# Block products for chunks 8 to 15 of the first MoE layer, and down-sampled attention in three groups of rows

## The chip, the cores and the metric

The kernel runs on one core of a Trainium2 chip. The metric is the device time of one execution, in microseconds (us), from the first to the last instruction of the program and what little lies around them. TensorE (PE) multiplies, ScalarE (ACT) and VectorE (DVE) do the element work, GpSimd (POOL) a few sums, SyncE (SP) issues every DMA.

## What is computed

```python
# q, k, v: [2 batches, 8 heads, 576 positions, 64]
q_d, k_d, v_d = means over 4 neighbouring positions          # 144 rows a head
out_d     = softmax(q_d @ k_d.T / 8) @ v_d                    # down-sampled attention
out_local = softmax(q @ k.T / 8 where |i - j| < 4) @ v        # window attention
x = (repeat(out_d, 4) + out_local) as [1152 tokens, 512]
h = x @ w_in                       # 512 -> 2048     first MoE layer
x = (h * tanh(softplus(h))) @ w_out                  # 2048 -> 512
g, val = x @ w_gate, x @ w_val     # 512 -> 1536     second MoE layer
out = (g * sigmoid(g) * val) @ w_out2                # 1536 -> 512
```

The weights come as 64-bit floats, the rest as 32-bit floats.

## The kernel before

All operations are first recorded in a `Plan`, each with its engines, its costs in us, its dependencies and a due time (`want`); `Plan.run` then lists them in time order by these costs, and that list is the order of the instructions on every engine. The table `STEER` shifts the due times of single operations. Nothing is reordered on the chip: each engine goes through its list and waits where an operand is not ready. Where PE has nothing ready in the plan before 95 us, `run` puts a filler matmul there (`warm`, 256 columns of a constant, its result unused).

**Attention.** Heads go in pairs: `p` 0 to 3 in batch `b`. `prep` loads `qk` (queries and keys), `vq` (values for the down-sampled part) and once a batch `qr` (the last 64 positions), transposes on PE and sums four neighbours. `down` is the down-sampled attention of a pair: `score` (PE), `mx`, `neg` (DVE), `exps` (ACT), `norm`, `weigh`, `turn` (PE transposes of the probabilities), `ev`, `values`, `keep`. The 144 rows of each of the two heads stood as two halves of 72 rows, so four groups on 72 partitions. `duo` is the window attention of two units of 192 tokens; there are twelve, its last PE step is `o_local`, and it needs the windows `vw` (`load_windows`, four loads of a set). `dma` allows six loads in flight (`DEPTH`): each waits for the sixth before it.

**Matrix products.** Every factor is split into a high and a low part, and each product is three matmuls (`mm3`: high by high, high by low, low by high). Tokens go in three pieces of 384 (`PIECES`). The 2048 columns of the first layer are 16 chunks of 128; `l1(f, i)` is chunk `f` on piece `i`: 4 x 3 matmuls of 384 columns. `convert` loads a weight chunk (`raw`) and turns 64-bit floats into the two parts in `wt` (8 buffers): `fold`, `field` on ACT, `join` on DVE, `hi` on either, `lo` on DVE. `mish` works on two or four chunks `H` at once and leaves `G`. `l2` multiplies four chunks by `w_out`, twelve groups a block, and sums into `yacc`. The order is chunks 0 to 7, `l2` of block 0, chunks 8 to 11, `l2` of block 1, chunks 12 to 15, and so on.

**Block products.** The second layer (`l3`) already takes its chunks in pairs, and pieces 0 and 1 by seven products of blocks instead of eight (`products`). For that `combine` makes two more weight tiles of a pair from sums of halves (`sw`), and `turn_tokens` makes four token tiles (`tok` and a part of `yb`) from differences of blocks. A product is 2 x 3 matmuls; `keep` and `add_` move and add its result. Piece 2 is done plainly.

Of the kernel before, what the change touches and what calls it, by code (L numbers as in the profile page):

```python
# [8 lines left out]
F32 = mybir.dt.float32  # L9
# [18 lines left out]
PC = 384  # L28
# [5 lines left out]
DEPTH = 6  # L34
FLIGHT = 5
STEER = {
# [62 lines left out]
class Op:  # L99
    def __init__(self, eng, fn, deps, want, new, use, table):  # L100
        self.eng, self.fn, self.want, self.new, self.use, self.table = eng, fn, want, new, use, table
        self.left, self.at, self.out, self.end = 0, 0.0, [], None
        self.rings = {id(x.ring): x.ring for x in self.new}.values()
        for d in deps:
            if d is not None:
                self.left += 1
                d.out.append(self)
        for x in self.use:
            x.left += 1


class Plan:
# [5 lines left out]
    REST, SHARE, REACH, LAND = 0.0, 1.3, 1.5, 0.5  # L118
# [11 lines left out]
    def run(self):  # L130
# [10 lines left out]
        while todo:  # L141
            later, ran = [], False
            for e in names:
# [33 lines left out]
                if e == "DVE" and free["POOL"] > now:  # L177
                    d *= self.SHARE
# [37 lines left out]
def attention_moe_kernel(  # L216
# [259 lines left out]
    def prep(b, p, w):  # L476
# [39 lines left out]
        l_v = [plan.add({E_SP: us_dma(288, 1024, 12)}, ld_v, [], w - 5, [vq])]  # L516
# [72 lines left out]
    def down(b, p, qkd, vd, o_d, o_v, w):  # L589
# [4 lines left out]
        ed = buf(wk, [72, 2, 2, SD], F32, "ed", 2)  # L594
        md = buf(wk, [72, 2, 2, 2], F32, "md", 3)
        ptd = buf(wk, [72, 2, 2, SD], F32, "ptd", 1)
        old = ups.get("op")

        def score(e):
            for y in ba + [ed, md]:  # L600
                y.make()
            for c in range(2):
                for h in range(2):
                    hh = slice(64 * h, 64 * h + 64)
                    PE.matmul(out=ba[h].tile[0:72, SD * c:SD * c + SD], lhsT=qkd.tile[hh, 0, 72 * c:72 * c + 72],  # L605
# [714 lines left out]
```

## Time and profile before

| | |
|---|---|
| median of 3 runs | 492.81 us (492.2 to 496.83) |
| profiled execution | 495.21 us, of it 493.4 us span |
| PE busy | 483.1 us, 98% of the span |
| DVE busy | 327.3 us, 66% |
| ACT busy | 267.7 us, 54% |

The span is from the first to the last instruction of the profiled execution. Busy shares are over the whole span; the stages differ, and the rows further down are read by stage.

### The profile page before, as it was taken

The numbers are of one execution on the slowest core, as the hardware profiler recorded it, in microseconds if no ns is written. First come the engines' busy times: TensorE is split into PE (matmuls) and PEld (weight loads), VectorE is DVE, ScalarE is ACT, GpSimd is POOL, SyncE is SP. The second block draws the span as 40 slices with busy tenths as digits, with TensorE's granted clock in tenths as the row PEclk, the third lists the DMA queues.
The fourth block names the chain that finished last, engine by engine and source line by source line (L and its number), as shares of the span: only waits on it lengthen the run. The fifth ranks groups of instructions, "written<-read, shape, count | busy, mean of one in ns | idle before, by whom it ended". The sixth has DMA issues, their size and how long they took to land.

```text
span 493.4 us, 9431 instructions
## 1 busy us (share of the span) xinstructions
PE 483.1 (98%) x3857; PEld 454.2 (92%) x3857; DVE 327.3 (66%) x634; ACT 267.7 (54%) x523; POOL 21.5 (4%) x41
## 2 busy tenths in 40 slices
PE   9999799999999999999999999999999999999996
PEld 6777589999999999999999999999998899998885
DVE  4989869639504643865578989798892298872522
ACT  3677668669627733867252775666661485730000
POOL 2333210000000000000000000000000000000000
PEclk9999979999999999999999999999999999999999
DMA  8999996622300640153111051423351042400022
GB/s 169 171 178 187 190 159 181 207 86 86 128 1 0 182 161 1 43 177 123 43 31 55 2 166 48 128 63 111 97 182 62 0 115 101 126 4 0 0 108 85
DMA packets 59993, 48.79 MB, mean 99 GB/s; under 512 B 32430, under 2 KB 55214, under 8 KB 59950
## 3 DMA queue, kind: packets, MB, share of 16 engines
q1 hardware_dynamic: 59950, 48.19, 38.0%
q8 instruction: 30, 0.49, 0.4%
q14 instruction: 13, 0.11, 0.1%
HBM read 45.83 MB, written 2.36 MB: 98 GB/s over the span
## 4 chain that ended last, share of the span: by engine, by line
PE 94%; DMA 4%; issue 1%; DVE 0%; SPq 0%
PE b L850 23%; PE b L852 23%; PE b L851 23%; PE b L1145 5%; PE b L1144 5%; PE b L1146 5%; DMA vw<-in_v_dram 3%; PE warm L1283 2%; PE b L789 2%; DMA qr<-in_k_dram 1%; PE b L540 1%; PE b L746 1%; PE b L605 1%; PE b L656 1%; PE b L776 1%; PE b L644 1%
## 5 line engine op out<-in xcount | busy, mean ns | idle before, releaser
L850 PE MATMUL b<-xy,wt 128*128 128x384 f32 x384 | 129.7, 338 | 0.0
L852 PE MATMUL b<-xy,wt 128*128 128x384 f32 x384 | 128.7, 335 | 0.0
L851 PE MATMUL b<-xy,wt 128*128 128x384 f32 x384 | 128.7, 335 | 0.0
L850 PEld LDWEIGHTS b<-xy,wt 128*128 128x128 f32 x384 | 72.3, 188 | 0.7 <-ACT cw L351 0.4
L851 PEld LDWEIGHTS b<-xy,wt 128*128 128x128 f32 x384 | 72.4, 189 | 0.0
L852 PEld LDWEIGHTS b<-xy,wt 128*128 128x128 f32 x384 | 72.3, 188 | 0.0
L852 PE MATMUL b<-G,wt 128*128 128x384 f32 x192 | 64.7, 337 | 0.0
L850 PE MATMUL b<-G,wt 128*128 128x384 f32 x192 | 64.6, 336 | 0.0
L851 PE MATMUL b<-G,wt 128*128 128x384 f32 x192 | 64.3, 335 | 0.0
L272 ACT ACTIVATE H<-b 128x384 f32<-128x384 f32 x60 | 29.3, 488 | 59.0 <-PE b L852 58.8
L358 DVE SCALAR_TENSOR_TENSOR cw<-raw,cw 128x512 uint32<-128x512 uint32 x68 | 46.5, 685 | 13.2 <-ACT cw L355 12.7
L351 ACT ACTIVATE cw<-raw 128x512 f32<-128x512 int8 x68 | 45.3, 667 | 17.9 <-DVE wt L372 12.5
L372 DVE TENSOR_TENSOR wt<-cw,wt 128x512 fp32r<-128x512 f32 x68 | 46.2, 685 | 5.5 <-ACT wt L272 4.0
L274 DVE CAST wt<-cw 128x512 fp32r<-128x512 f32 x29 | 12.3, 423 | 51.4 <-PE b L851 31.9
L355 ACT ACTIVATE cw<-cw 128x512 int32<-128x512 f32 x68 | 42.7, 628 | 1.0
L1145 PE MATMUL b<-wt,G 128*128 128x512 f32 x108 | 42.3, 392 | 0.0
L1144 PE MATMUL b<-wt,G 128*128 128x512 f32 x108 | 42.2, 391 | 0.0
L1146 PE MATMUL b<-wt,G 128*128 128x512 f32 x108 | 42.1, 390 | 0.0
L851 PEld LDWEIGHTS b<-G,wt 128*128 128x128 f32 x192 | 36.0, 188 | 0.0
L850 PEld LDWEIGHTS b<-G,wt 128*128 128x128 f32 x192 | 36.0, 188 | 0.0
L852 PEld LDWEIGHTS b<-G,wt 128*128 128x128 f32 x192 | 36.0, 188 | 0.0
L965 DVE TENSOR_TENSOR acc<-b,acc 128x384 f32<-128x384 f32 x36 | 19.6, 553 | 23.7 <-PE b L852 23.7
(108 smaller groups left out, 743.0 us busy)
## 6 DMA issues: line engine op xcount, KB each, us to landing
raw<-in_moe_w_out_dram SPq DMA_DIRECT2D x28, 512.0 KB
raw<-in_moe_w_in_dram SPq DMA_DIRECT2D x16, 512.0 KB
raw<-in_moe_w_gate_dram SPq DMA_DIRECT2D x12, 512.0 KB
raw<-in_moe_w_val_dram SPq DMA_DIRECT2D x12, 512.0 KB
vw<-in_v_dram SPq DMA_DIRECT2D x14, 189.0 KB
vq<-in_v_dram SPq DMA_DIRECT2D x8, 288.0 KB
out_dram<-acc SPq DMA_DIRECT2D x9, 256.0 KB
qk<-in_q_dram SPq DMA_DIRECT2D x8, 256.0 KB
```

The source lines that it names most:

```text
L272: ACT.activation(out, in_, AF.Copy)
L351: ACT.activation(cw.make(), raw.tile[:, 8:4104].bitcast(I8).rearrange("p (n b) -> p n b", b=8)[:, :, 0], AF.Prelu, scale=-1.0, bias=-56.0, ...
L355: ACT.activation(cw.tile.bitcast(I32), cw.tile, AF.Prelu, scale=-2.0 ** 27 / SLOPE, bias=-112 * 2.0 ** 27, alpha=SLOPE)
L358: DVE.scalar_tensor_tensor(out=cw.tile.bitcast(U32), in0=raw.tile[:, 0:4096].bitcast(U32).rearrange("p (n b) -> p n b", b=2)[:, :, 1], sca ...
L372: DVE.tensor_tensor(out=wt.tile[:, 1], in0=cw.tile, in1=wt.tile[:, 0].bitcast(F32), op=ALU.subtract)
L850: PE.matmul(out=ps, lhsT=wt_hi, rhs=m_hi, start=first, stop=False, **more)
L851: PE.matmul(out=ps, lhsT=wt_hi, rhs=m_lo, start=False, stop=False, **more)
L852: PE.matmul(out=ps, lhsT=wt_lo, rhs=m_hi, start=False, stop=last, **more)
L965: DVE.tensor_tensor(out=ya, in0=ps.tile[:, 0:n], in1=ya, op=ALU.add)
L1144: PE.matmul(out=ps.tile, lhsT=g[:, 0, tok], rhs=wt[:, 0], start=(f == fs[0]), stop=False)
L1145: PE.matmul(out=ps.tile, lhsT=g[:, 0, tok], rhs=wt[:, 1], start=False, stop=False)
L1146: PE.matmul(out=ps.tile, lhsT=g[:, 1, tok], rhs=wt[:, 0], start=False, stop=(f == fs[-1]))
```

## The change

Chunks 8 to 15 of the first layer (`PAIRS = 8`) go in four pairs by seven products on pieces 0 and 1 (`l1_pair`), with the same `products` as the second layer, now told where its tokens are. `turn_x` makes the four token tiles: it adds the two parts of `x` back together (four DVE additions of 768 columns into the buffer `acc`), subtracts (four), and splits again (four `hi`, four `lo`); one of the four overwrites piece 1 of two rows of `x`, once chunks 0 to 7 have read it. Each pair of chunks has its `combine`. In `down`, the 288 rows of the two heads now stand in three groups of 128 partitions: 80 rows of the first head, then its other 64 beside 64 of the second head, then the second head's other 80. The first and the third group carry 48 rows that nothing reads. The load of `vq` is two transfers, of 64 and of 8 partitions. `STEER` and the plan's cost of sharing (`SHARE`, now on four kinds of DVE operations alone) are other numbers.

```diff
+PAIRS = 8
-    REST, SHARE, REACH, LAND = 0.0, 1.3, 1.5, 0.5
+    REST, SHARE, REACH, LAND = 0.0, 1.5, 1.5, 0.5
+    SHARED = ("norm_l", "x_lo", "lo", "join")
...
-            dma(out=vq.make().rearrange("p h c f -> p (h c) f"),
-                              in_=bass.AP(tensor=s_.tensor, offset=s_.offset, ap=[[4 * D, 72], [2 * SD * D, 4], [1, 4 * D]]))
+            vq.make()
+            for r, n in ((0, 64), (64, 8)):
+                dma(out=vq.tile.rearrange("p h c f -> p (h c) f")[r:r + n],
+                    in_=bass.AP(tensor=s_.tensor, offset=s_.offset + 4 * D * r, ap=[[4 * D, n], [2 * SD * D, 4], [1, 4 * D]]))
...
-            for h in range(2):
-                for c in range(2):
-                    ACT.activation(ed.tile[:, h, c], ba[h].tile[0:72, SD * c:SD * c + SD], AF.Exp, bias=md.tile[:, 0, h, c:c + 1],
-                                   scale=1.0 / 16.0, accum_out=md.tile[:, 1, h, c:c + 1])
+            for g in range(3):
+                ACT.activation(ed.tile[:, g], group(g), AF.Exp, bias=md.tile[:, 0, g:g + 1], scale=1.0 / 16.0, accum_out=md.tile[:, 1, g:g + 1])
...
-                for a in range(2):
-                    for c in range(2):
-                        PE.transpose(out=ba[h].tile[0:72, SD * a + 72 * c:SD * a + 72 * c + 72], in_=ed.tile[:, h, c, 72 * a:72 * a + 72],
-                                     identity=ident[:72, :72])
+                for g, (a, n) in enumerate(rows):
+                    PE.transpose(out=ba[h].tile[0:72, a:a + n], in_=ed.tile[0:n, g, 72 * h:72 * h + 72], identity=ident[:n, :n])
...
+    def turn_x(want):
...
+        for x, (r, c) in enumerate(((0, 0), (0, 1), (1, 1), (1, 0))):
+            def back(e, x=x, r=r, c=c):
+                if x == 0:
+                    xacc.make()
+                hi, lo = [xt[:, z, 2 * r:2 * r + 2, (p0, p1)[c]].bitcast(F32) for z in range(2)]
+                DVE.tensor_tensor(out=part(x), in0=hi, in1=lo, op=ALU.add)
...
+        for x, a, b in ((0, 1, 0), (1, 2, 1), (2, 2, 0), (3, 3, 2)):
+            def sub_(e, x=x, a=a, b=b):
+                DVE.tensor_tensor(out=part(x), in0=part(a), in1=part(b), op=ALU.subtract)
...
+            later = [] if t else reads
+            o = plan.add({"ACT": us_act(2 * PC), "DVE": us_ts(2 * PC)}, hi, [subs[k]] + later, want, [t] if t else [], [xacc] + ([] if t else [x_buf]))
+            xtok_ops.append(plan.add({"DVE": us_tt(2 * PC)}, lo, [o] + later, want, use=[xacc, t or x_buf]))
...
+    def l1_pair(f, want):
...
+        tokens = (x_buf, lambda: xt, raw, t, xtok_ops, [x_buf] + xtok)
+        pa, o4, c11, c12, c22 = products("1", f, want, hs, both, tokens)
+        tail = [cols_group("1", f + x, 2, lambda: xt, [o for p in range(NP) for o in x_ops[p, 2]], want + x, [x_buf]) for x in range(2)]
...
     def add_l1(fs):
+        if fs[0] >= PAIRS:
+            for f in fs[::2]:
+                groups.append(([("1", f, 2)], 5.82, lambda t, f=f: l1_pair(f, t)))
+            return
...
     add_l1((6, 7))
+    groups.append(((), 0, lambda t: turn_x(t - 12.0)))
```

**SP's list around the last loads of attention.** In the kernel before, from the last query load on (`qk` queries and keys, `vq` and `vw` values, `raw` weight chunks of the first layer):

```order
L279 DMA qk_143<-in_q_dram 128x8x64
L279 DMA vq_152<-in_v_dram 72x4x256
L279 DMA qk_143<-in_k_dram 128x8x64
L279 DMA vw_270<-in_v_dram 42x18x64 x4
L279 DMA vq_156<-in_v_dram 72x4x256
L279 DMA raw_1052<-in_moe_w_in_dram 128x4x1024
L279 DMA raw_1092<-in_moe_w_in_dram 128x4x1024
L279 DMA raw_479<-in_moe_w_in_dram 128x4x1024
L279 DMA vw_200<-in_v_dram 42x18x64 x3
```

The same place in the changed kernel:

```order
L281 DMA qk_143<-in_q_dram 128x8x64
L281 DMA qk_143<-in_k_dram 128x8x64
L281 DMA vw_578<-in_v_dram 42x18x64 x3
L281 DMA vw_316<-in_v_dram 42x18x64
L281 DMA vq_171<-in_v_dram 64x4x256
L281 DMA vq_171<-in_v_dram 8x4x256
...
L281 DMA raw_973<-in_moe_w_in_dram 128x4x1024
L281 DMA raw_1017<-in_moe_w_in_dram 128x4x1024
L281 DMA vw_316<-in_v_dram 42x18x64 x2
L281 DMA vw_316<-in_v_dram 42x17x64
...
L281 DMA vw_578<-in_v_dram 42x18x64 x4
```

Three windows `vw` and one `vq` that stood ahead of the last key load now stand behind it, and two weight chunks instead of three stand in front of the last windows (one more stands far ahead of this place in both).

**PE's list at the first matmuls of the first layer.** Before, behind the seventh of the twelve `o_local` (L789; L644 and L776 transposes, L605 scores of the down-sampled attention, `xy` the tokens):

```order
L789 MATMUL b_219<-pt_435,vw_270 64x32 x2
L776 MATMUL b_224<-ident,exs 128x128 x3
L605 MATMUL b_182<-qkd_234 72x144
L605 MATMUL b_193<-qkd_234 72x144
...
L850 MATMUL b_225<-xy_82,wt_734 128x384
L851 MATMUL b_225<-xy_82,wt_734 128x384
```

In the changed kernel, behind the sixth (L795; L742 and L752 scores of the windows):

```order
L795 MATMUL b_218<-pt_581,vw_578 64x32 x2
L742 LDWEIGHTS identb
L742 MATMUL b_181<-masks,identb 128x228
L752 MATMUL b_181<-qkT_211 32x38 x10
L752 MATMUL b_181<-qkT_211 32x35 x2
L856 MATMUL b_237<-xy_82,wt_688 128x384
L857 MATMUL b_237<-xy_82,wt_688 128x384
```

The first layer begins one window group earlier; up to the last `o_local` 120 of its matmuls stand instead of 72. In the whole list 84 fillers stand instead of 117, 48 transposes of `turn` instead of 64, and 1920 matmuls of 384 columns instead of 1944.

**DVE's list behind the last window group.** Before, from the last token split on (`xy<-xs`; L358 `join`, L372 `lo`):

```order
L813 TENSOR_TENSOR xy_82<-xs_696,xy_82 128x2x192
L358 SCALAR_TENSOR_TENSOR cw_1268<-raw_1052,cw_1268 128x512
L274 CAST wt_1532<-cw_1335 128x512
L372 TENSOR_TENSOR wt_1532<-cw_1335,wt_1532 128x512
L274 CAST wt_734<-cw_685 128x512
L372 TENSOR_TENSOR wt_734<-cw_685,wt_734 128x512
```

In the changed kernel (L951, L959 and L973 are `back`, `sub_` and `lo` of `turn_x`):

```order
L819 TENSOR_TENSOR xy_82<-xs_728,xy_82 128x2x192
L951 TENSOR_TENSOR acc_1688<-xy_82 128x768 x4
L959 TENSOR_TENSOR acc_1688<-acc_1688 128x768
L374 TENSOR_TENSOR wt_1505<-cw_1159,wt_1505 128x512
L276 CAST wt_1465<-cw_643 128x512
L959 TENSOR_TENSOR acc_1688<-acc_1688 128x768
L374 TENSOR_TENSOR wt_1465<-cw_643,wt_1465 128x512
L276 CAST wt_1206<-cw_1134 128x512
L959 TENSOR_TENSOR acc_1688<-acc_1688 128x768
```

`turn_x` stands at once behind the last split, between the conversions of weights; in PE's list the first product on a token tile of `turn_x` stands 192 matmuls behind the last `o_local`, and the first matmul of `l2` 222 behind it.

## Rows read from the trace of the kernel before

**Rows 1.** The page: span, granted clock, DMA share and rate in 40 slices.

```profile
span 493.4 us, 9431 instructions
...
PEclk9999979999999999999999999999999999999999
DMA  8999996622300640153111051423351042400022
GB/s 169 171 178 187 190 159 181 207 86 86 128 1 0 182 161 1 43 177 123 43 31 55 2 166 48 128 63 111 97 182 62 0 115 101 126 4 0 0 108 85
```

**Rows 2.** Windows: stretch, length, each engine's busy time (instructions), clock, DMA, GB/s.

```profile
100.00:125.00 25.00, 25.00 (x147) 25.00 (x146) 17.48 (x28) 20.84 (x25) 0.00 (x0) 1.00 0.27 85
125.00:150.00 25.00, 25.00 (x144) 25.00 (x143) 5.31 (x7) 9.33 (x19) 0.00 (x0) 1.00 0.19 64
150.00:175.00 25.00, 25.00 (x146) 25.00 (x145) 15.61 (x24) 18.89 (x30) 0.00 (x0) 1.00 0.35 109
...
275.00:300.00 25.00, 25.00 (x145) 25.00 (x145) 23.57 (x49) 18.57 (x33) 0.00 (x0) 1.00 0.28 85
```

**Rows 3.** Windows around the stretch of lower clock, columns as in rows 2.

```profile
61.00:64.00 3.00, 3.00 (x64) 2.42 (x60) 0.84 (x3) 1.28 (x4) 1.99 (x3) 0.50 1.06 273
64.00:68.00 4.00, 4.00 (x29) 3.24 (x24) 2.64 (x8) 1.97 (x4) 0.18 (x1) 0.53 1.04 130
```

**Rows 4.** Chain that ended last, in order of time: start, us, what.

```profile
8.42 0.87 PE warm L1283 x8
...
57.02 2.15 issue
59.17 0.59 PE b L789 x25
...
66.25 0.62 PE b L850
...
88.17 0.83 PE b L789 x48
```

**Rows 5.** Groups by form: line, engine, operation, names, shapes, count, busy us, mean ns.

```profile
L1283 PE MATMUL warm<-wsrc 128*128 128x256 bf16 x117 | 18.9, 304 | 1.1 <-DVE wsrc L454 1.1
...
L644 PE MATMUL b<-ident,ed 72*72 72x72 f32 x64 | 6.7, 241 | 0.0
```

**Rows 6.** Timeline of SP's DMA issues: start, us, what.

```profile
46.08 0.61 SPq L279 DMA_DIRECT2D qk<-in_k_dram  x1
...
54.98 2.98 SPq L279 DMA_DIRECT2D raw<-in_moe_w_in_dram  x3
59.73 8.73 SPq L279 DMA_DIRECT2D vw<-in_v_dram  x6
```

**Rows 7.** Groups by form on DVE, columns as in rows 5.

```profile
L372 DVE TENSOR_TENSOR wt<-cw,wt 128x512 fp32r<-128x512 f32 x68 | 46.2, 685 | 5.5 <-ACT wt L272 4.0
...
L908 DVE TENSOR_TENSOR G<-H,G 128x1152 fp32r<-128x1152 f32 x16 | 21.0, 1350 | 0.0
...
L274 DVE COPY H<-b 128x384 f32<-128x384 f32 x24 | 13.1, 554 | 12.8 <-PE b L852 12.6
...
L274 DVE CAST wt<-cw 128x512 fp32r<-128x512 f32 x29 | 12.3, 423 | 51.4 <-PE b L851 31.9 <-PE b L1146 19.3
L274 DVE CAST G<-H 128x1152 fp32r<-128x1152 f32 x16 | 11.7, 752 | 0.5 <-PE b L1145 0.4
...
L394 DVE TENSOR_TENSOR sw<-cw 128x256 f32<-128x256 f32 x12 | 5.0, 416 | 0.1
...
L1012 DVE TENSOR_TENSOR H<-acc 128x768 f32<-128x768 f32 x2 | 1.9, 954 | 0.0
```

**Rows 8.** Timeline of DVE in a run without waits: start, us, what.

```profile
110.26 0.75 DVE L274 CAST G<-H 128x1152 fp32r<-128x1152 f32 x1
110.93 0.69 DVE L372 TENSOR_TENSOR wt<-cw,wt 128x512 fp32r<-128x512 f32 x1
111.53 1.35 DVE L908 TENSOR_TENSOR G<-H,G 128x1152 fp32r<-128x1152 f32 x1
```

More of the change, by code (lines that the diff above doesn't have):

```diff
@@ L601, in score @@
                 y.make()
[L602 to L606 removed]
+            t = qkd.tile.rearrange("p a j -> p (a j)")
+            for h in range(2):
+                hh = slice(64 * h, 64 * h + 64)
+                PE.matmul(out=ba[h].tile[:, 0:SD], lhsT=t[hh, 64 * h:64 * h + 128], rhs=t[hh, SD:2 * SD], start=True, stop=True)
+            for h in range(2):
+                hh = slice(64 * h, 64 * h + 64)
+                PE.matmul(out=ba[0].tile[hh, SD:2 * SD], lhsT=t[hh, 80 * (1 - h):80 * (1 - h) + 64], rhs=t[hh, SD:2 * SD], start=True, stop=True)
+        group = lambda g: (ba[0].tile[:, 0:SD], ba[0].tile[:, SD:2 * SD], ba[1].tile[:, 0:SD])[g]
+        rows = ((0, 80), (80, 128), (208, 80))
         def mx(h):
             def f(e):
[L610 removed]
+                n = 2 - h
+                DVE.tensor_reduce(out=md.tile[:, 0, 2 * h:2 * h + n], in_=ba[h].tile[:, 0:SD * n].rearrange("p (c j) -> p c j", c=n),
                                   axis=AX.X, op=ALU.max)
@@ L870, in cols_group @@
         o = plan.add({E_PE: 6 * us_mm(n)}, part(0), list(deps) + [wt_ops[kind, f]], want, [ps] + list(new), [wts[kind, f]] + list(use))
+        if kind == "1" and i == 1:
+            reads.append(o)
         o = plan.add({E_PE: 6 * us_mm(n)}, part(1), [o], want, use=[ps, wts[kind, f]] + list(use))
@@ L926, in attention_moe_kernel, with hi, lo @@
     batch, sizes = [], list((2, 2, 2, 2, 4, 4))
+    xtok = [buf("g", [128, 2, 2, PC], F32R, "tok%d" % x, 1) for x in range(3)]
+    xtok_ops = []
+    xacc = buf("acc", [128, 4, NTOK], F32, "acc", 1)
+    def turn_x(want):
+        p0, p1 = [slice(c0, c0 + n) for c0, n in PIECES[:2]]
+        part = lambda x: xacc.tile.rearrange("p a n -> p (a n)")[:, 2 * PC * x:2 * PC * x + 2 * PC].rearrange("p (c n) -> p c n", c=2)
+        whole = []
+        for x, (r, c) in enumerate(((0, 0), (0, 1), (1, 1), (1, 0))):
[4 more added lines that the diff above has]
+                DVE.tensor_tensor(out=part(x), in0=hi, in1=lo, op=ALU.add)
+            deps = [o for p in (2 * r, 2 * r + 1) for o in x_ops[p, c]] + att_ops
+            whole.append(plan.add({"DVE": us_tt(2 * PC)}, back, deps + whole[:1], want, [] if x else [xacc], [x_buf] + ([xacc] if x else [])))
+        last = list(whole)
+        subs = {}
+        for x, a, b in ((0, 1, 0), (1, 2, 1), (2, 2, 0), (3, 3, 2)):
+            def sub_(e, x=x, a=a, b=b):
+                DVE.tensor_tensor(out=part(x), in0=part(a), in1=part(b), op=ALU.subtract)
+            deps = whole + [subs[k] for k in ((), (0,), (0, 1), (2,))[x]]
+            subs[x] = plan.add({"DVE": us_tt(2 * PC)}, sub_, deps, want, use=[xacc])
+        for x, k in enumerate((0, 2, 1, 3)):
+            t = xtok[x - 1] if x else None
+            dest = (lambda z, t=t: t.tile[:, z]) if x else lambda z: xt[:, z, 0:2, p1]
+            def hi(e, k=k, dest=dest, t=t):
+                if t:
+                    t.make()
+                copy(e, dest(0), part(k))
+            def lo(e, k=k, dest=dest):
+                DVE.tensor_tensor(out=dest(1), in0=part(k), in1=dest(0).bitcast(F32), op=ALU.subtract)
+            later = [] if t else reads
+            o = plan.add({"ACT": us_act(2 * PC), "DVE": us_ts(2 * PC)}, hi, [subs[k]] + later, want, [t] if t else [], [xacc] + ([] if t else [x_buf]))
+            xtok_ops.append(plan.add({"DVE": us_tt(2 * PC)}, lo, [o] + later, want, use=[xacc, t or x_buf]))
     yacc = buf("acc", [128, 4, NTOK], F32, "acc", 1)
@@ L1027, in turn_tokens, with products @@
             tok_ops.append(o)
-    def products(kind, f, want, home, hold):
+    def products(kind, f, want, home, hold, tokens):
+        place, tile, raw, t, t_ops, t_bufs = tokens
         n = PC
@@ L1072, in products, with evac, fn @@
         c22 = add_(pc, hold.slots[2], [o5, k3])
-        o4 = product(pa, (kind, f + 1), 1, t[3], [tok_ops[3], k3], False, True, [tok[2]])
-        o3 = product(pc, (kind, f, 1), 1, y(1, 1), raw[2] + [c22], False, True, [yb])
+        o4 = product(pa, (kind, f + 1), 1, t[3], [t_ops[3], k3], False, True, t_bufs[3:4])
+        o3 = product(pc, (kind, f, 1), 1, y(1, 1), raw[2] + [c22], False, True, [place])
         c12 = add_(pc, hold.slots[1], [o3, k2])
         return pa, o4, c11, c12, c22
+    def l1_pair(f, want):
+        plan.at = None
+        p0, p1, p2 = [slice(c0, c0 + n) for c0, n in PIECES]
+        hs = [buf(thp, [128, NTOK], F32, "H", RING) for _ in range(2)]
+        both = Buf(ring(None, "hold", 99))
+        both.slots = [lambda: hs[0].tile[:, p0], lambda: hs[0].tile[:, p1], lambda: hs[1].tile[:, p1]]
+        raw = {0: [o for p in (0, 1) for o in x_ops[p, 0]], 1: [o for p in (2, 3) for o in x_ops[p, 0]], 2: [o for p in (2, 3) for o in x_ops[p, 1]]}
+        t = [lambda z, j: xt[:, z, j, p1]] + [lambda z, j, x=x: xtok[x].tile[:, z, j] for x in range(3)]
+        tokens = (x_buf, lambda: xt, raw, t, xtok_ops, [x_buf] + xtok)
+        pa, o4, c11, c12, c22 = products("1", f, want, hs, both, tokens)
+        tail = [cols_group("1", f + x, 2, lambda: xt, [o for p in range(NP) for o in x_ops[p, 2]], want + x, [x_buf]) for x in range(2)]
+        def evac(h, cs, ps, deps):
+            def fn(e):
+                copy(e, h.tile[:, cs], ps.tile[:, 0:PC])
+            return plan.add({"ACT": us_act(PC, True), "DVE": us_tt(PC)}, fn, deps, want - 4, use=[ps, h])
+        first = c11
+        for x in range(2):
+            h = HB[f + x] = hs[x]
+            h.ops = [evac(h, p2, tail[x][0], [tail[x][1], first])] + ([c11, c12] if x == 0 else [c22, evac(h, p0, pa, [o4])])
+        for x in range(2):
+            mish(f + x, hs[x], want)
```

61 lines of the change are left out of this document (29 added, 32 removed), and 51 rows, old and new, of the table STEER.

## The prediction

> **What bounds the kernel now.** I read the windows first, because the average hides two stages. From 100 us on PE is busy 25.00 of every 25 us at full clock, with 144 to 147 matmuls in each window [rows 2]: it never waits, so what is cut from its list there comes off the time one for one. 145 matmuls of 384 columns in 25 us [rows 2] make 0.172 us each; I use this distance, not the duration of one, since matmuls overlap. The first 90 us are the other stage, attention. There the DMA engines are full: 8 or 9 tenths in each of the first six slices at 159 to 190 GB/s, with shares of 1.06 and 1.04 in the windows around 64 us [rows 1, 3]. PE fills what it cannot use with 117 fillers [rows 5], and still stands 2.15 us at 57 us, a wait for which the profile names no releaser [rows 4]. Soon after, the granted clock is 0.50 (1.2 GHz) from 61 to 64 us and 0.53 on the mean from 64 to 68 [rows 3]: 3 x 0.50 + 4 x 0.47 = 3.4 us of PE's time lost. So the time is the list of dense matmuls plus what the loads and these waits leave of the first 90 us.
>
> The profiled execution has a span of 493.4 us [rows 1], and its own time lies 2.4 us above the median of the runs shown. I make the sum on the span and take the difference off the median, 492.81.
>
> **Part 1: fewer dense matmuls.** A pair of chunks took 2 x 2 x 12 = 48 matmuls on pieces 0 and 1 and takes 7 x 6 = 42; four pairs save 24. 24 x 0.172 = **-4.1 us**, and nothing covers it, since PE is full where they stood [rows 2]. Both ends are near this value if PE stays fed.
>
> **Part 2: fillers.** 33 fillers fewer stand in PE's list. Eight of them take 0.87 us on the chain [rows 4], 0.109 each: 33 x 0.109 = -3.6 us if PE has something else to do then, and 0 if it stands instead. What decides is when the loads land. Up to the last key load the changed SP list has three windows (189 KB each) and one `vq` (288 KB) fewer in front, 855 KB; at 180 GB/s, the middle of the first five slices [rows 1], that is 4.9 us. In the kernel before that load is issued at 46.08 [rows 6], so its place should now be reached near 41. The last windows have one weight chunk (512 KB, 2.9 us) fewer in front; before, they are issued from 59.73 on, behind three chunks [rows 6]. Both gains are of the size of the fillers taken out, so I take **-3.6**.
>
> One rule speaks against the split of `vq`: the Trainium skill, "DMA: Bandwidth & Descriptors", section "Bandwidth", says that transfers under 64 KB are dominated by their descriptors, and the new piece of 8 partitions is 32 KB. No row here has such a load of values alone. What it would do is the first rival below, priced from rows.
>
> **Part 3: the down-sampled attention.** PE's transposes in `turn` go from 64 to 48. Their busy time is 6.7 us in all [rows 5], about 0.1 each; but 16 of the 48 are now wider (128 rows for 72). Between 0 and -1.6, nearest to the low end since they are still bound by columns: **-0.5**. ACT has 8 exponentials fewer and DVE 8 narrower maxima. Neither engine is on the path there (the DMA engines are), so this is worth nothing by itself; it is cover for the fact that the same steps now have to run some us earlier.
>
> **Part 4: the wait at 57 us and the half clock.** Together 2.15 + 3.4 = 5.5 us [rows 3, 4]. The new list has another set of windows and other matmuls at that time, and the first layer, which begins at 66.25 [rows 4], begins one window group sooner, so PE has more at hand. But the wait has no named releaser, so it may well come back elsewhere, and new places are tight: the first `o_local` again stands behind four window loads of which the last has a weight chunk in front of it. From 0 to -5.5; nothing speaks for either end, so I take half, **-2.7**.
>
> **Part 5: what is added on DVE and ACT.** It has to hide beside PE. `turn_x` is 12 DVE operations of 768 columns at 0.954 [rows 7] = 11.4 us and four `hi`; each `combine` adds 4 x 0.416 + 2 x 0.685 = 3.0 us on DVE and two `hi`; a pair has 3 more results to move or add, at 0.554 [rows 7] 1.7 us. Over four pairs that is 11.4 + 12.1 + 6.6 = 30 us of DVE. Between 100 and 175 us DVE is busy 17.5, 5.3 and 15.6 of 75 [rows 2], so there is room on the mean; and in the second layer DVE is busy 23.57 of 25 beside a full PE [rows 2], so such a load alone does not stop PE.
>
> The tight place is the first one. Between the last window group and the first matmul of `l2` stand 222 dense matmuls: 222 x 0.172 = 38.3 us for PE. In DVE's list the same stretch (to the `lo` of the first `G` that `l2` reads) has 52 operations: 12 of 768 columns (11.4), 13 `join` or `lo` of 512 (13 x 0.685 = 8.9), 5 casts of 512 (2.1), 3 casts of 1152 (2.3), 5 `lo` of 1152 (6.8), 9 of 384 (5.0), 4 of 256 (1.7), one split (0.6): 38.8 us by their durations [rows 7]. But a DVE operation starts before the record of the one ahead ends: 110.26 to 110.93 is 0.67 for a record of 0.75, 110.93 to 111.53 is 0.60 for 0.69 [rows 8]. With 0.08 off each the list takes 34.6 us. That leaves 3.7 us for every wait that DVE has on ACT or PE in there. If these waits are longer, PE stands for the rest, one for one. I allow **+1.0**, with 0 and +5 as ends. Behind this stretch the four chunks of `l2` give each later pair cover again: DVE was nearly idle in such a block (5.31 of 25 [rows 2]).
>
> The `vq` loads cost eight more issues on SP; an issue there takes 0.61 us when it waits for nothing [rows 6]. SP otherwise waits for the sixth load before, so I cost this at nothing; the cover is the full DMA queue, and without it it would be 8 x 0.61 = 4.9 us.
>
> **Sum.** -4.1 - 3.6 - 0.5 - 2.7 + 1.0 = -9.9 us: a span near 483.5, and 492.8 - 9.9 = **483 us**.
>
> **Rivals.**
>
> *The first 90 us give nothing.* The loads gain 4.9 us by their order and lose 8 x 0.61 = 4.9 by their number, each small load also taking one of six places in flight. Then every filler taken out comes back as a wait, and the wait at 57 us with its half clock stays. What is left is -4.1 - 0.5 + 1.0 = -3.6: 489 us. For it: the DMA engines are already full [rows 1]. Against it: a full queue is bound by bytes, and the bytes in front are fewer. The fillers also keep PE active: the Trainium skill, "TensorE: Matmul & The Clock Gate", section "Part 1: The HAM clock gate (the warmup mystery)", says that the lower clock is the default and activity lifts it. The trace agrees as far as the clock fell only behind the wait [rows 3, 4]; by that rule a second such stretch would cost another 3.4 us, to 492.5.
>
> *The first 90 us give everything.* No wait like the one at 57 us, no half clock, part 3 at its low end, no stall later: -4.1 - 3.6 - 1.6 - 5.5 = -14.8, 478 us. For it: the order reaches all keys earlier. Against it: that wait has no named cause that the change removes.
>
> *DVE becomes the bound behind attention: slower.* The 52 operations have 3.7 us to spare. They hang on ACT, which swaps function tables several times there and has four 768-column copies of its own. If each of the 52 waits 0.4 us on the mean, that is 20.8 - 3.7 = 17 us of PE standing in pieces, with one stretch of half clock behind it (3.4): -9.9 - 1.0 + 17 + 3.4 = +9.5, 502 us. It decides for slower than before once the stall passes 10.9 us. Against it: PE took no wait at all in the second layer under the same kind of load [rows 2].
>
> **Chances.** The forecast, 479 to 488, has 0.62; the front giving nothing 0.18, of which most falls within 1% of before; the front giving everything 0.14; DVE as the bound, slower, 0.06. A difference of 1%, 4.9 us, is about what a measurement of this kernel can tell from no change. Faster by over 1% (below 487.9): nearly all of the forecast, the third case and a little of the second, 0.77. Within 1%: 0.17. Slower: 0.06. The range for 8 in 10 runs from 476.5, just past the case in which all is won, to 489.5, the middle of the case in which the front gives nothing.
>
> **What would show it.** Right: PE at 25.00 of 25 us from about 95 us on, 24 dense matmuls fewer, the first matmul of the first layer near 55 to 58 us instead of 66.25, and the last `o_local` again near 88.17 [rows 4], but with 120 dense matmuls in front of it instead of 72. Wrong in part 2: PE waits of several us on loads before 60 us. Wrong in part 4: the clock at 0.50 for some us again. Wrong in part 5: PE idle between 100 and 140 us, waiting for DVE's `turn_x` or `sw` operations. The prediction falls if PE shows a clear share of waits in the block products, which I take to cost nothing.

## The result: 489.81 us, and the first 100 us gave next to nothing

The changed kernel takes 489.81 us (median of 20, 487.22 to 492.5), the kernel before 493.29 (20 runs, 490.9 to 500.05): a ratio of 0.9917, 95% interval 0.9893 to 0.9941. That is 3.5 us by the medians and 4.6 by the means (95%: 3.2 to 6.1), where 9.9 were forecast. A ratio, here and below, compares the executions within 1.5% of their kernel's fastest, so it leaves out more of a kernel whose times spread more; medians and means are over all. The profiled execution took 492.18 us, 490.4 of it span.

The page of the changed kernel answers to [rows 1]: span, granted clock, DMA share and rate, and the instruction queues.

```profile
span 490.4 us, 9324 instructions
...
PEclk9997997999999999999999999999999999999999
DMA  9999993613222151073211041323351042400022
GB/s 173 181 160 190 190 175 121 217 43 100 72 87 87 43 172 43 2 243 101 87 43 44 16 156 51 123 86 93 119 175 43 1 129 88 130 0 0 1 107 86
...
q8 instruction: 29, 0.48, 0.4%
```

The lower clock is there twice, in the fourth and the seventh slice; before it was there once, in the sixth [rows 1]. The windows, columns as in [rows 2]:

```profile
25.00:50.00 25.00, 22.64 (x465) 17.52 (x465) 18.39 (x55) 15.43 (x54) 8.65 (x12) 0.86 0.98 174
...
75.00:100.00 25.00, 23.43 (x303) 21.99 (x304) 15.94 (x36) 14.88 (x29) 0.00 (x0) 0.86 0.53 168
100.00:125.00 25.00, 25.00 (x145) 25.00 (x144) 24.03 (x37) 20.07 (x29) 0.00 (x0) 1.00 0.20 68
125.00:150.00 25.00, 25.00 (x145) 25.00 (x145) 20.32 (x33) 23.18 (x32) 0.00 (x0) 1.00 0.28 86
150.00:175.00 25.00, 25.00 (x146) 25.00 (x145) 11.05 (x19) 14.34 (x26) 0.00 (x0) 1.00 0.23 65
```

Behind 100 us all is as predicted: PE is full, beside a DVE that is busy 24.03 and 20.32 of 25 us where it was 17.48 and 5.31 [rows 2]. From the last `o_local` to the last dense matmul the trace has 2196 dense matmuls in 400.25 us before and 2124 in 387.32 now. 48 of the 72 now stand ahead of that `o_local`, where 120 are done instead of 72; 24 are gone. What is missing is missing in front. The chain, in order of time, as [rows 4]:

```profile
28.42 7.51 DMA vw<-in_v_dram
35.97 0.89 PE b L795 x46
...
65.10 7.22 DMA vw<-in_v_dram
72.36 1.41 PE b L795 x81
73.77 2.80 issue
76.57 0.53 PE b L795 x8
...
98.05 0.83 PE b L795 x48
```

L795 is `o_local`. The last one starts at 98.05 where 88.17 was expected; the 48 more dense matmuls ahead of it explain 8.3 us of the 9.9 later. Two long waits stand in the chain: 1.99 us on a window load, until 35.97, and 2.80 us with no releaser, until 76.57. The PE waits by cause (us in total, times, longest) and the windows behind the two:

```profile
PE b L795 <- issue: 2.8, 1, 2.8
PE b L795 <- DMA vw<-in_v_dram: 2.3, 2, 2.0
```

```profile
38.00:41.00 3.00, 3.00 (x18) 2.17 (x15) 2.97 (x11) 2.17 (x10) 0.00 (x0) 0.50 0.78 204
41.00:44.00 3.00, 3.00 (x59) 2.50 (x58) 1.66 (x5) 1.58 (x4) 2.12 (x4) 0.50 1.01 213
...
76.00:79.00 3.00, 2.43 (x36) 1.98 (x40) 1.69 (x4) 1.03 (x3) 0.00 (x0) 0.50 0.03 5
79.00:82.00 3.00, 3.00 (x52) 2.92 (x43) 2.10 (x5) 2.49 (x7) 0.00 (x0) 0.50 0.57 177
```

Each time the granted clock is 0.50 (1.2 GHz). The clock's records give 37.74 to 44.57 and 75.29 to 82.11 us: 13.65 us at half clock, 6.8 us lost, against 3.4 before. The loads did come earlier, as SP's timeline shows beside [rows 6]: the last key load at 42.34 instead of 46.08, the last windows from 55.68 instead of 59.73.

```profile
42.34 1.34 SPq L281 DMA_DIRECT2D qk<-in_k_dram  x1
...
55.68 10.04 SPq L281 DMA_DIRECT2D vw<-in_v_dram  x9
65.82 16.42 SPq L281 DMA_DIRECT2D raw<-in_moe_w_in_dram  x5
```

Counted from one matmul's end to the next up to the last `o_local`, the fillers take 12.81 us (84) instead of 16.67 (117): the 3.9 us that part 2 forecast. Waits over 0.25 us take 6.79 instead of 6.11, the dense matmuls 23.2 (120) instead of 14.0 (72), and the attention's own instructions 56.1 instead of 52.2. Together these are the 9.9 us. Of the 3.9 us that the attention's own instructions gained, the second stretch of half clock explains up to 2.5 (an estimate: its 3.4 us less the 0.9 by which the dense matmuls exceed 8.3).

### The profile page after: what moved, and what is told of

It reads as the page before. It is cut to its first block, busy times and chain, and to the rows that moved or that the text cites. A ratio compares the mean times of both kernels' runs of the same rounds, so it can differ in the third digit from the quotient of the medians.

```text
span 490.4 us, 9324 instructions
## 1 busy us (share of the span) xinstructions
PE 479.2 (98%) x3784; PEld 448.9 (92%) x3784; DVE 348.1 (71%) x675; ACT 274.0 (56%) x518; POOL 21.1 (4%) x41
## 4 chain that ended last, share of the span: by engine, by line
PE 93%; DMA 3%; DVE 2%; issue 1%; SPq 0%; ACT 0%
PE b L856 23%; PE b L858 22%; PE b L857 22%; PE b L1220 5%; PE b L1221 5%; PE b L1219 5%; DMA vw<-in_v_dram 3%; PE b L795 2%; PE warm L1363 2%; PE b L544 2%; PE b L752 1%; PE b L782 1%; PE b L662 1%; PE b L651 1%; PE b L609 1%
## 5 line engine op out<-in xcount | busy, mean ns | idle before, releaser
L856 PE MATMUL b<-xy,wt 128*128 128x384 f32 x352 | 119.6, 340 | 0.0
L858 PE MATMUL b<-xy,wt 128*128 128x384 f32 x352 | 118.3, 336 | 0.0
L857 PE MATMUL b<-xy,wt 128*128 128x384 f32 x352 | 118.2, 336 | 0.0
L856 PEld LDWEIGHTS b<-xy,wt 128*128 128x128 f32 x352 | 66.5, 189 | 0.7 <-issue 0.2
L857 PEld LDWEIGHTS b<-xy,wt 128*128 128x128 f32 x352 | 66.5, 189 | 0.0
L858 PEld LDWEIGHTS b<-xy,wt 128*128 128x128 f32 x352 | 66.4, 189 | 0.0
L360 DVE SCALAR_TENSOR_TENSOR cw<-raw,cw 128x512 uint32<-128x512 uint32 x68 | 46.6, 687 | 10.1 <-ACT cw L357 9.8
L274 ACT ACTIVATE G<-H 128x1152 fp32r<-128x1152 f32 x16 | 18.2, 1165 | 50.3 <-PE b L858 28.3
L276 DVE CAST wt<-cw 128x512 fp32r<-128x512 f32 x26 | 11.0, 423 | 36.6 <-PE b L1221 19.3
```

What stands on the lines that cost most here:

```text
L274: ACT.activation(out, in_, AF.Copy)
L276: DVE.tensor_copy(out=out, in_=in_)
L360: DVE.scalar_tensor_tensor(out=cw.tile.bitcast(U32), in0=raw.tile[:, 0:4096].bitcast(U32).rearrange("p (n b) -> p n b", b=2)[:, :, 1], sca ...
L856: PE.matmul(out=ps, lhsT=wt_hi, rhs=m_hi, start=first, stop=False, **more)
L857: PE.matmul(out=ps, lhsT=wt_hi, rhs=m_lo, start=False, stop=False, **more)
L858: PE.matmul(out=ps, lhsT=wt_lo, rhs=m_hi, start=False, stop=last, **more)
```

## The experiments

All are timed beside the kernel before on the same chip. Every execution gives its span and mean granted clock, so each span can be split: span x (1 - clock) is **lost to half clock**, and what is left is **the rest**. Over 121 executions of the kernel before (12 of them e_again), on five chips, the span grows by 0.92 us per us lost (compared within chips), so this loss is nearly all on the path. It is also part of how the kernel before differs between chips (medians of 493.3 to 500.5 us, mean losses of 4.7 to 7.7), so kernels are compared within a chip; the changed kernel itself was timed only on the first chip and on C. A mean span of 6 or 12 executions is known to within some 1 to 3 us in most rows (95%). One part of the loss stays in the rest: in the traces the clock's records begin only 3.9 to 7.0 us into the span, and until then the fillers stand 0.21 us apart instead of 0.11. Of the changed kernel's chain, whose records begin at 7.02:

```profile
1.05 5.73 PE warm L1363 x26
...
8.75 0.87 PE warm L1363 x8
```

| chip, kernel | fillers | n | mean span | lost | rest | ratio (95%) |
|---|---|---|---|---|---|---|
| first: changed kernel | 84 | 20 | 488.0 | 5.4 | 482.7 | 0.9917 (0.9893-0.9941) |
| A: before | 117 | 17 | 493.8 | 5.3 | 488.5 | |
| A: e_nopairs | 84 | 12 | 492.1 | 4.7 | 487.4 | 1.0017 (0.9981-1.0053) |
| A: e_win | 84 | 6 | 488.6 | 6.3 | 482.3 | 0.9889 (0.9843-0.9936) |
| A: e_late | 84 | 6 | 488.2 | 5.9 | 482.3 | 0.9871 (0.9808-0.9933) |
| A: e_both | 84 | 6 | 488.1 | 4.7 | 483.4 | 0.9878 (0.9822-0.9935) |
| B: before | 117 | 35 | 495.5 | 6.1 | 489.4 | |
| B: e_again (before) | 117 | 12 | 494.4 | 5.2 | 489.2 | 1.003 (0.9979-1.008) |
| B: e_nofill | 26 | 12 | 489.0 | 11.2 | 477.9 | 0.9927 (0.9869-0.9985) |
| B: e_morefill | 117 | 12 | 488.5 | 4.1 | 484.4 | 0.9902 (0.9849-0.9954) |
| B: e_down4 | 84 | 12 | 489.5 | 8.5 | 481.0 | 0.9931 (0.9877-0.9985) |
| C: before | 117 | 23 | 493.6 | 4.7 | 488.9 | |
| C: e_after2 (changed) | 84 | 6 | 488.6 | 4.7 | 483.8 | 0.9873 (0.9798-0.9949) |
| C: e_thin (before) | 84 | 12 | 496.5 | 10.5 | 486.0 | 1.0113 (1.0073-1.0152) |
| C: e_fill2 | 142 | 6 | 488.9 | 2.7 | 486.2 | 0.9898 (0.9826-0.997) |
| C: e_both_more | 117 | 12 | 489.0 | 3.4 | 485.6 | 0.9946 (0.9904-0.9988) |
| D: before | 117 | 11 | 498.4 | 7.7 | 490.7 | |
| D: e_aimed | 116 | 6 | 488.9 | 2.8 | 486.1 | 0.9817 (0.9766-0.9868) |
| D: e_nofill_aimed | 62 | 6 | 487.9 | 6.3 | 481.7 | 0.9798 (0.9754-0.9841) |
| D: e_late_aimed | 116 | 6 | 490.0 | 4.4 | 485.6 | 0.9809 (0.9761-0.9857) |
| D: e_vq1 | 84 | 6 | 489.8 | 4.9 | 484.9 | 0.9835 (0.979-0.988) |
| E: before | 117 | 23 | 494.6 | 6.0 | 488.6 | |
| E: e_depth4 | 84 | 12 | 492.5 | 8.4 | 484.1 | 0.998 (0.9942-1.0018) |
| E: e_nofill_depth4 | 62 | 12 | 492.7 | 10.1 | 482.6 | 0.9966 (0.9928-1.0005) |

In the diffs, `order` is the planner's finished list, `at(name, k)` the place in it of the k-th call of a function (from 0), and `behind(i, j)` moves entry i behind entry j. Unless named otherwise the kernel is the changed one.

### The block products alone (e_nopairs)

```diff
-PAIRS = 8
+PAIRS = 16
-    groups.append(((), 0, lambda t: turn_x(t - 12.0)))
```

> The changed kernel with chunks 8 to 15 done plainly (eight block products, no token tiles, no sums of weights); its list up to 90 us is untouched. Theory W (the first 100 us eat the gain: two PE waits, 1.99 us at 34 us and 2.80 us at 74 us, each with 6.8 us of half clock behind it): the 24 matmuls come back at 0.172 each, so 4.1 us more than the changed kernel, 493.9 against 489.8, and level with the kernel before. Theory P (the block products cost DVE and ACT what they save PE): no more than the changed kernel, 489 to 490.

Measured: 1.0017, and 1.7 us less by the mean spans (within the noise of 2.2). With the changed front but no block products the kernel takes about as long as before; on the same chip it stands 3.5 to 4.1 us over e_win, e_late and e_both, which have them (taken together 3.9, 95%: 2.5 to 5.2). The median, 494.01 us, is theory W's 493.9. So the block products are worth their 24 matmuls, theory P falls, and what the front gains is not clear of the noise: 1.0 us of rest (487.4 against 488.5), give or take 1.6.

### The two waits (e_win, e_late, e_both)

```diff
 e_win, e_both
+        behind(at("convert.<locals>.load", 0), at("load_windows.<locals>.f", 3))
 e_late, e_both (the fourth chunk's load also waits for the last matmul of that o_local)
+        for n in (5, 4, 3):
+            behind(at("convert.<locals>.load", n), at("duo.<locals>.o_local", 6))
```

> The changed kernel with one exchange in SP's list: the first weight chunk (512 KB) goes behind the fourth window load of the first set instead of in front of it. Theory W: PE's wait at 34 us (1.99 us) falls below 0.5 and the half clock behind it (3.4 us) goes too: 2 to 5 us less than the changed kernel, 485 to 488. Theory L (the first 60 us are bound by bytes, so a wait taken away comes back at the next load): the wait moves to the next key load near 38 us, 489 to 490.

> The changed kernel with the fourth to sixth weight chunk issued only when the first of the three window groups near 72 us is done on PE; before, they are issued from 65.8 us on. PE's list is untouched. Theory I (the 2.80 us wait at 74 us, for which the profile names no releaser, is PE waiting for its next block of instructions, whose transfer is queued behind these chunks): the wait and its half clock go, 2.8 + 3.4 less, 483 to 486; the chunks are then up to 5 us later, which may give 1 us back. If the wait is for data of attention or for another engine: it stays, 489 to 491.

> Both exchanges together. Theory W with I: both waits and both half-clock stretches go, 7 to 11 us less than the changed kernel, 479 to 483. Theory L: 488 to 491, the waits only change places.

Measured: 0.9889, 0.9871 and 0.9878, on one chip; the intervals overlap with each other and with the changed kernel's. The median times, 490.07, 488.52 and 489.42 us, reach none of the ranges of theories W and I; the first and the third lie at theory L's. The waits aimed at went, others came. Of e_late, PE's waits by cause:

```profile
PE b L870 <- ACT xy L281: 2.1, 1, 2.1
PE b L568 <- DMA qr<-in_q_dram: 1.4, 1, 1.4
```

The 2.80 us have become 2.1 on a piece of `x` at 77 us, the 1.99 us 1.4 on a load of queries at 31 (`qr`, the last positions), and the mean loss is 5.9 us. Of e_both:

```profile
PE b L871 <- ACT xy L282: 1.4, 1, 1.4
```

So taking the named waits away one by one is worth little.

### Fillers (e_again, e_nofill, e_morefill, e_thin, e_fill2)

```diff
 all, ahead of the loop that issues the list
+        first = min(i for i, x in enumerate(order) if x[2] == "PE" and x[1] is not self.spare[0])
+        fill = [i for i, x in enumerate(order) if i > first and x[1] is self.spare[0]]
 e_nofill: the 58 behind the first real PE instruction out
+        order[:] = [x for i, x in enumerate(order) if i < first or x[1] is not self.spare[0]]
 e_morefill: 33 more (e_fill2: 58 more)
+        for n, i in enumerate(reversed(fill)):
+            order[i:i] = [order[i]] * (33 * (n + 1) // len(fill) - 33 * n // len(fill))
 e_thin, in the kernel before: 33 out
+        drop = {i for k, i in enumerate(fill) if 33 * (k + 1) // len(fill) > 33 * k // len(fill)}
+        order[:] = [x for i, x in enumerate(order) if i not in drop]
```

e_again is the kernel before, e_after2 the changed kernel, both unchanged.

> The kernel before once more, unchanged. All theories expect a ratio of 1.000 within 0.003. It is run for its clocks: twenty executions of the changed kernel have a mean granted clock of 0.980 to 0.997, which is 5.4 us of span lost to half clock on the mean (span times one minus clock). Theory C (the fillers hold the clock up, and 33 fewer of them let it fall more often) expects the kernel before to lose clearly less, near the 3.4 us of its one profile. Theory L (the front is set by loads and the steps that hang on them, and the clock falls in whatever waits are there) expects about the same 5 us.

> The changed kernel with the 58 fillers that stand behind the first real PE instruction taken out, everything else in the same order. Theory F (the prediction's part 2: fillers stand on PE's path) expects 58 x 0.109 = 6.3 us less than the changed kernel, a ratio of 0.979. Theory L expects each of them to come back as a wait: within 1 us of the changed kernel, 0.990 to 0.994. Theory C expects more half clock and a loss of 3 to 7 us against the changed kernel, a ratio of 0.998 to 1.006.

> The changed kernel with 33 fillers more, spread over the places where fillers stand already, so 117 as in the kernel before. Theory F expects 3.6 us more than the changed kernel, a ratio of 0.999. Theory L expects them to fit into waits: within 1 us, 0.990 to 0.994. Theory C expects the clock to hold better, a mean loss of 3.4 us instead of 5.4, and 1 to 2 us less than the changed kernel, a ratio of 0.987 to 0.990.

> The changed kernel once more, beside the kernel before on the same chip, with the clocks of every execution of both, so that each time can be split into the part lost to half clock (span times one minus clock) and the rest. Theory B (fillers do two things that cancel: each takes some 0.08 us of PE's path, and 33 fewer let the clock fall more) expects the rest to be 6 to 7 us under the kernel before (4.1 of it the dense matmuls, 2.5 the fillers), the loss 2 to 3 us over it, and a ratio near 0.992. Theory L (the front is set by loads, the fillers never mattered) expects the rest to be 4.1 us lower, the same loss, and also 0.992.

> The kernel before with 33 of its fillers taken out, spread evenly over all that stand behind the first real PE instruction, everything else in the same order: part 2's count alone. The prediction (33 x 0.109 us on PE's path) expects 3.6 us less, a ratio of 0.9927. Theory B expects the rest without the half clock to fall by 2.5 us and the loss to half clock to rise by about as much: 0.997 to 1.003. Theory L expects no difference in either part.

> The changed kernel with every filler behind the first real PE instruction twice (58 more). If fillers only stand on the path: 58 x 0.109 = 6.3 us over the changed kernel, 1.0045. Theory B expects the rest to rise by 3 to 5 us and the loss to half clock to fall from some 5 to 2 or 3: 0.991 to 0.996. Theory L expects them to fit into waits, with no change in either part.

The kernel before once more (e_again) loses 5.2 us, and 6.1 in the 35 executions beside it, about the 5.4 of the changed kernel, as theory L expects: theory C's 3.4 did not come.

Part 2 done alone is a loss. e_thin is slower than the kernel before, 1.0113 by the ratio and 2.9 us by the mean spans (95%: 0.9 to 4.8): the rest falls by 2.9 us, 0.088 for each filler, near the forecast 0.109, but the loss to half clock rises from 4.7 to 10.5 us. Its PE waits:

```profile
PE b L661 <- issue: 2.1, 1, 2.1
PE b L751 <- issue: 1.4, 1, 1.4
PE b L794 <- DMA vw<-in_v_dram: 1.3, 1, 1.3
```

The granted clock on the pages of e_thin, e_nofill and e_fill2:

```profile
PEclk9998879999999999999999999999999999999999
```

```profile
PEclk9886999999999999999999999999999999999999
```

```profile
PEclk9999999999999999999999999999999999999999
```

Fewer fillers, a lower clock; with 142 it did not fall in the profiled execution before the last matmuls' end. e_nofill against e_morefill, 91 fillers apart, differ by 6.5 us of rest one way and 7.1 us of loss the other, and their spans by 0.6. So theory F falls, and theory B holds for the fillers by themselves. It fails in one point: e_after2 loses no more than the kernel before beside it (4.7 both), where 2 to 3 us more were expected. Its rest is 5.0 us lower (95%: 3.7 to 6.4), not 6 to 7; over the 26 executions of the changed kernel with known clocks and the 121 of the kernel before it is 6.2 lower. With 4.1 of that the dense matmuls, the front's rest gained some 1 to 2 us.

e_morefill shows the change with part 2 undone, at the 117 fillers of the kernel before: 488.5 us against 495.2 over the 47 executions of the kernel before on that chip, 6.7 us less (95%: 4.9 to 8.6). Taking the 33 out as well gave no more: the changed kernel is 4.6 and 5.0 us under the kernel before on its two chips, and its mean spans there (488.0, 488.6) are within 0.5 us of e_morefill's. e_both_more, further down, also with 117, is 4.6 us under the kernel before (95%: 2.6 to 6.7).

### The number of fillers or their place (e_both_more, e_aimed, e_nofill_aimed, e_late_aimed)

```diff
 e_aimed (e_late_aimed: the same on e_late; e_both_more: e_both with e_morefill's lines)
+        fill = next(x for x in order if x[1] is self.spare[0])
+        for k in (8, 7, 6, 0):
+            i = at("duo.<locals>.o_local", k)
+            order[i:i] = [fill] * 8
 e_nofill_aimed, on e_nofill
+        for name in ("t_main.<locals>.f", "turn.<locals>.f"):
+            i = at(name, 6)
+            order[i:i] = [fill] * 18
```

> The changed kernel without its two named waits (as e_both: the first weight chunk behind the fourth window load, the fourth to sixth weight chunks behind the seventh o_local) and with 33 fillers more in the places that have some (as e_morefill). Theory B expects the clock to hold better than in e_both, a loss near 3 us, and a ratio of 0.984 to 0.988. If waits only change places, whatever is hidden or filled, 0.989 to 0.992.

> The changed kernel with 32 fillers more, 8 each directly ahead of the first, seventh, eighth and ninth o_local, where its profile shows PE's two long waits. If a filler ahead of a wait costs nothing and holds the clock (place decides): the loss to half clock falls from some 5 to 2 or 3 us, the rest stays near 483, a ratio of 0.984 to 0.988. If only their number counts, as e_morefill: a loss near 4.1, a rest near 484.4, 0.988 to 0.992.

> e_nofill with 18 fillers ahead of each of the two instructions at which its profile waits over 2 us (the transposes of the fourth pair of q, a wait on its load of 2.34 us at 16.07, and the seventh turn, a wait of 2.22 us at 29.5): 62 fillers in all, against 84 in the changed kernel. If place decides: the rest near 479, the loss down from 11.2 to some 5, a ratio of 0.980 to 0.986. If only their number counts: loss near 8 and rest near 480.5, 0.988 to 0.993.

> e_late (the fourth to sixth weight chunks behind the seventh o_local, with which the wait of 2.8 us at 74 us went) with the 32 fillers of e_aimed. If both hold: a loss of 3 us and a ratio of 0.982 to 0.986, the best so far. If the waits only change places: a loss near 5 and 0.987 to 0.991.

e_both_more lost 3.4 us, as theory B expects, but its rest is 485.6 beside e_both's 483.4, and its ratio, 0.9946, misses the forecast 0.984 to 0.988. The ratios on chip D look better since the kernel before takes longer there (498.4 us on the mean); the spans, 487.9 to 490.0 us, are near the changed kernel's elsewhere. e_aimed lost 2.8 us, as "place decides" expects, but its rest is 486.1 beside the 484.9 of e_vq1, which has 32 fillers fewer: nothing shows that they were free there, though a difference of 1.2 is within the noise. e_late_aimed lost 4.4 us, near what "waits change places" expects. e_nofill_aimed has the lowest span of the study by a hair, with a loss and a rest (6.3 and 481.7 us) that neither of its theories forecast; its two waits went, and 1.99 us without a releaser came at 74.5 us. No version tried is clearly faster than the changed kernel.

### Parts of the attention and its loads (e_down4, e_vq1)

```diff
 e_down4: score, mx, neg, exps, norm, weigh, turn, ev and values as in the kernel before, costs kept
-        ed = buf(wk, [128, 3, SD], F32, "ed", 2)
+        ed = buf(wk, [72, 2, 2, SD], F32, "ed", 2)
 e_vq1
-            for r, n in ((0, 64), (64, 8)):
+            for r, n in ((0, 72),):
```

> The changed kernel with the down-sampled attention in four groups of 72 rows again, all lists otherwise in the same order. The prediction's part 3 expects 0.5 us more than the changed kernel (16 narrow transposes more, less the width of the others), a ratio of 0.993. If its exponentials and maxima lie on the path (8 exponentials of some 0.36 us each, one per pair of heads' step), it expects up to 2.9 us more, 0.998. If three groups save nothing on PE, as PE's time for the scores suggests (5.54 us before, 6.06 after), 0.992.

> The changed kernel with each load of values as one transfer of 72 partitions again (eight transfers fewer), every list otherwise in the same order. The prediction costs the split at nothing: a ratio within 0.003 of the changed kernel's. If the eight small transfers hold the front up (its first rival, up to 4.9 us): 0.982 to 0.988. If one transfer of 72 partitions lands later than two: slower than the changed kernel, 0.995 or more.

Neither decides much. Four groups give 0.9931, with the forecasts of all theories inside its interval (rest and loss move against each other again: 481.0 and 8.5 us, beside 482.7 and 5.4 of the changed kernel on the first chip). One transfer per load of values gives 0.9835, in the band of the rival, but so do all kernels on that chip, where the kernel before takes longer. Beside them its span, 489.8 us for 487.9 to 490.0, is no gain, so there is no sign that the split holds the front up; the changed kernel itself was not timed on that chip.

### Where PE waits for nothing named (e_depth4, e_nofill_depth4)

The waits marked "issue" stand at a few numbers of PE's instructions, whatever stands there. Counting matmuls and weight loads from 0, number 2729 is a matmul of `o_local` in the changed kernel and in e_vq1, and one of the scores in e_nofill and e_nofill_aimed; in other versions of the changed kernel 1203, 1457, 2221 and 2475 recur, and neighbours among them are 254 apart. The wait at 57 us in the kernel before is at number 2215. Waits of e_vq1, then of e_nofill_aimed:

```profile
PE b L795 <- issue: 2.9, 1, 2.9
```

```profile
PE b L760 <- issue: 2.0, 1, 2.0
```

The page's queue q8 moves 29 packets, 0.48 MB, 16 KB each, one for every 261 of PE's 7568 matmuls and weight loads. In the steady part of the changed kernel's trace one comes every 228 to 290 PE instructions; near 74 us one is taken up at 74.17 us for 1.12, while weight chunks issued from 65.82 us on are being loaded and PE already stands, and PE goes on at 76.57. All 28 waits without a releaser over 0.25 us, in all traces, end like this one, 1.25 to 1.84 us behind the end of a packet of q8 (for the wait at 57 us, 1.64). So PE waits there for a block of its own instructions.

```diff
-        if len(loads) >= DEPTH:
-            tc.add_manual_dep(i.ins, loads[-DEPTH].ins.name,
+        if len(loads) >= 4:
+            tc.add_manual_dep(i.ins, loads[-4].ins.name,
```

> The changed kernel with four loads in flight instead of six (each load waits for the fourth before it), every list in the same order. If PE's waits without a releaser are fetches of its instructions that stand behind loads in flight: no such wait over 0.5 us at its instructions 2221, 2475 and 2729, a loss to half clock of 3 us or less unless waits on loads take their place, and a ratio to the kernel before like or below that of the changed kernel (0.987 to 0.992 on two other chips). If the depth of six was needed to keep the DMA engines full: more waits on named loads, and slower than the changed kernel, 0.995 or more. If these waits have another cause, they stay where they are.

> e_nofill_aimed (62 fillers) with four loads in flight instead of six. There the wait without a releaser at instruction 2729 was 2.0 us. If fetches behind loads cause it, it goes, the loss falls from 6.3 to some 4 us, and the ratio is 0.003 to 0.006 under that of e_depth4. If not, the same ratio as e_depth4 within 0.003.

With four loads in flight no wait over 0.25 us without a releaser is left in either profile, as the theory of late instruction fetches expects. But e_win, e_late and e_fill2 have none either, with six, and waits on loads took their place (of e_depth4):

```profile
PE b L795 <- DMA vw<-in_v_dram: 2.4, 2, 1.4
...
PE b L555 <- DMA qr<-in_q_dram: 0.9, 1, 0.9
```

The waits on `vw` stand just ahead of number 2729, at 2563 and 2567, and cover the fetch: the block is taken up at 75.63 us, 8.6 us behind the one before, where the changed kernel took 7.7. By this measure fewer loads in flight did not bring it sooner. In e_late, with three weight chunks issued later, it came at 72.17, 4.1 us behind the one before, when PE was at 2448, and PE did not stop; but e_win, with the chunks where they were, took 5.0 us. That the block stands behind data loads is thus possible, but not shown.

The losses to half clock are 8.4 and 10.1 us, and the kernel 0.998 of the one before: the depth of six is needed, and e_nofill_depth4 was not better by more than its interval.

## Why the prediction was wrong

- **Part 1 was right.** 24 matmuls less, 4.1 us: e_nopairs against the variants of the changed kernel beside it gives 3.5 to 4.1.
- **Part 2 failed.** It priced the 33 fillers at -3.6 us, with 0 as the worst end "if it stands instead". The measured worth is nothing or a loss. With the 33 put back (e_morefill) the kernel is 6.7 us under the one before, and the sum without part 2 is -6.3; without them it is 4.6 and 5.0 under it on other chips, so taking them out gained nothing that these runs can tell. e_thin, the same number taken out alone, is slower than before: their 2.9 us are had, and 5.8 us of half clock come for them. The prediction did name the rule that activity holds the clock, but in a rival, at one stretch of 3.4 us, and left it out of the bound of this term. That bound should have reached above zero. The Trainium skill, "TensorE: Matmul & The Clock Gate", "Part 1: The HAM clock gate (the "warmup" mystery)", shows, under "HAM oscillation", a kernel whose waits on DMA make the clock fall again and again, and counts the time at half clock as half lost. The runs agree with that price: 0.92 us of span per us so counted.
- **Part 4 gave little.** The wait at 57 us did go, and 1.99 us at 34 and 2.80 us at 74 came, the first with half clock behind it, the second with half clock from its middle on. Over the executions with known clocks the changed kernel loses 5.2 us (26) and the kernel before 5.8 (121): of the 2.7 us taken, some 0.5, give or take 1.3. At equal fillers (e_morefill) the loss is 4.1 for 5.9, so part of the gain may have been there and been spent on the fillers that are gone.
- **Part 3's -0.5 isn't seen.** Counted from one matmul's end to the next, PE's scores, which the term left out, take 6.7 us instead of 5.6 in the two traces, and its transposes 5.5 in both; e_down4's interval holds the forecasts of all its theories.
- **Part 5 was right in its mechanism, and its +1.0 was 0:** PE is at 25.00 beside DVE's 24.03.
- **The loads** came 3.7 and 4.1 us earlier, about as forecast (4.9 and 2.9), and that was not what the front waited for as a whole. My reading, which no single run isolates, is that PE's list, the loads and the clock stand so near each other that what one gives, another takes. The first rival, "the first 90 us give nothing", came about in its number, 489 us. Of its reasons, the number of loads finds no support (e_vq1), the wait at 57 us did not stay, and the fillers came back, as half clock more than as waits: so the number is in part luck.

Open: e_thin pays 5.8 us of clock for its 33 fillers, and the changed order does without them at no more loss than before (4.7 and 4.7 us). An order that loses less by itself would explain it, as e_morefill suggests (4.1 us for 5.9, a difference of 1.8, give or take 1.6), but the intervals are wide, and no run has the new order of the loads with everything else as before.

## What to carry to other kernels

An instruction that does no useful work can still be paid for: before counting a filler as a gain, take some out alone and look at the granted clock of every execution, not at one profile. Split each time into what half clock took and the rest; a change that moves both in opposite directions looks like no effect at all. And in a stretch where DMA engines and PE are both nearly full, price the removal of a wait by the next one behind it.

## What the runs showed of the hardware

PE can run out of instructions. Its waits without a releaser, up to 2.9 us, stood at a few instruction numbers, neighbours some 254 apart, and all 28 over 0.25 us ended 1.25 to 1.84 us behind a 16 KB packet of queue q8. What made a packet late is not shown.

The span's first 3.9 to 7.0 us ran at half pace in every trace (fillers 0.21 us apart, then 0.11), which the granted clock, counted from its first record, leaves out.

The half clock came behind waits of PE, or within one, with PE busy for most of the time around them, in stretches of 3.4 to 24 us. Mostly the longest wait shortly before it was of 0.7 to 3.9 us; before three stretches (one in e_win, two in e_thin) it was only 0.35 to 0.56 us, while waits of 0.9 and 1.0 us in the kernel before and 0.8 us in e_fill2 passed without it. The loss differed from execution to execution of one kernel: the kernel before had spans of 487.9 to 503.3 us in 121 executions, and its loss to half clock goes with them (correlation 0.89).
